# The last half chunk of batch 0 in a fused attention and feed-forward kernel: two TensorE transposes become DMA transposes, and its numerators move from step 10 to step 29

## The chip, the cores and the metric

The kernel runs on one core of a Trainium2 chip. The metric is the device time of one execution in microseconds (us). Nine executions of the kernel before gave a median of 250.71 us, from 249.87 to 252.09. One of them was taken by the hardware profiler; all views below are of that execution. TensorE is called PE (PEld is its weight load), VectorE is DVE, ScalarE is ACT, GpSimd is POOL and SyncE is SP.

## What is computed

Linear attention for 8 batches of 8 heads, 576 positions and 64 channels, and then a feed-forward net on the 4608 resulting tokens of width 512:

```python
theta = np.pi / 2.0 * pos / S
phi(x) = concat([relu(x) * cos(theta), relu(x) * sin(theta)])   # 128 features
kv  = einsum('bhsf,bhsd->bhfd', phi(k), v);  z = sum_s phi(k)
num = einsum('bhsf,bhfd->bhsd', phi(q), kv)
den = einsum('bhsf,bhf->bhs', phi(q), z) + 1e-6
x   = (num / den) transposed to [token, 512]
out = ((x @ w1) * (x @ w2)) @ w3 @ w_out
```

The kernel multiplies w3 and w_out once, into `w34b`, and uses that for all tokens.

## The kernel before, in words

**Tiling.** A batch's 576 positions are cut into five chunks: four of 128 rows and one of 64 rows, chunk 4, called the half chunk here. The tokens of all batches, in order, are cut into nine tiles of 512 for the feed-forward net. Batch 0 has 576 tokens, so its chunks 0 to 3 fill tile 0, and its half chunk is the first 64 columns of tile 1.

**What one chunk of queries goes through.** `features` (L258) makes the 128 features of each head in `qp`: DVE makes the cosine half (L263), ACT the sine half (L267). Then the features have to stand on the partitions: `q_tr` (L321) does it by eight PE transposes into PSUM (L326) and a copy into `qpT` (by DVE, L328, or by ACT, L329); in other places `prep_q` (L277) issues a DMA transpose from SP (L281). `num` (L343) multiplies the features with the batch's `kvs`, eight matmuls of 65 columns (L355) that give numerators and denominators in PSUM, and DVE divides: denominator (L371), reciprocal (L372), product (L373) into `xblk`. Last, `x_tr` (L391) turns `xblk` into the columns of `xT` that the net reads: by four PE transposes (L407) and a copy (L409), or by a DMA transpose from SP (L403), which batches from 2 on and chunk 3 of batch 1 use.

**What sets the order.** The program is laid out by hand. `ffn_groups(t)` (L446) is a generator for token tile t; it issues a group of PE work (four matmuls of 512 columns for the most part) and yields. After the g-th group everything in `slots[g]` is issued (L650 to L655), and `at(s, ...)` (L549) puts work there. Tile 0 has groups, or steps, 0 to 39. Steps 0 to 15 form the products with w1 and w2 (L452), steps 16 to 31 the product of w3 and w_out (`w34_mm`, L225, matmul L230), two steps for each of eight blocks `jp`; steps 32 to 39 the output product (L522). Tile 1 begins after step 39. Each engine runs its own instructions in the order in which they were issued, and waits by semaphores for what others give it. So a step number fixes the place in each engine's queue, not a time; an engine with nothing queued before an instruction can run it as soon as its data are there.

**Around the change.** The half chunk's features are made at step 6, `q_tr(0, 4)` stands at step 8, `num(0, 4)` at 10 and `x_tr(0, 4)` at 12 (L613 to L618). The transposes of the eight w3 blocks, `w3_tr` (L215, PE transposes L218 and a DVE copy L220), stand at steps 13, 15, 17, 19, 22, 24, 26 and 28 (L620); block 4 is the one at step 22. Batch 1's query features and its `q_tr` calls start at steps 29 and 31 (L623 to L626).

**Loads.** Nearly all loads are issued from POOL, and they convert float32 to bf16. `other_loads` (L197) issues the later ones in this order: the rest of w1 and w2, blocks 0 and 1 of w3, w_out, blocks 2 and 3 of w3, the keys of batch 1, then blocks 4 and 5 in one transfer and 6 and 7 in another (L142); step 7 adds queries and values of batch 1 and queries of batch 2 (L614). SP issues two loads of keys at the start and then nothing until batch 1's first DMA transpose at step 31.

Of the kernel before, what the change touches and what calls it, by code (L numbers as in the profile page):

```python
# [20 lines left out]
ROWS = [128, 128, 128, 128, 64]  # L21


def columns_of(b, c):


    if b % 2 == 0:
        return 128 * c
    return 0 if c == 4 else 64 + 128 * c


def out_rows(b, c):

    if c < 4:
        return slice(0, 128)
    return slice(64, 128) if b % 2 == 0 else slice(0, 64)
# [32 lines left out]
def kernel(  # L69
# [11 lines left out]
    nc = tc.nc  # L81
# [29 lines left out]
    def load(b, which, part=None):  # L111
        for name in which:
            src = {"k": k, "v": v, "q": q}[name]
            if part != 1:
                raw[b, name] = ld.tile([P, H, NCH, D], BF16, name=name + "s",
                                       bufs=2 if name == "q" else 1)
                nc.gpsimd.dma_start(
                    out=raw[b, name][0:64, :, :, :].rearrange("p h j d -> p h (j d)"),
                    in_=src[b, :, 0:320, :].rearrange("h (p j) d -> p h (j d)", j=5))
            if part != 0:  # L120
                nc.gpsimd.dma_start(
                    out=raw[b, name][64:128, :, 0:4, :].rearrange("p h j d -> p h (j d)"),
                    in_=src[b, :, 320:S, :].rearrange("h (p j) d -> p h (j d)", j=4))
# [25 lines left out]
    q0 = raw[0, "q"] = ld.tile([P, H, NCH, D], BF16, name="qs", bufs=2)  # L149
# [8 lines left out]
    def feature_buffers(i):  # L158

        va = const.tile([P, NCH, H, D + 2], BF16, name=f"va{i}")  # L160
        nc.vector.memset(va[:, :, :, D:D + 1], 1.0)
        nc.vector.memset(va[64:128, 4, :, 0:D], 0.0)
        va_bufs.append(va)
        for name, bufs in (("kp", kp_bufs), ("qp", qp_bufs)):
            fp = const.tile([P, NCH, H, F], BF16, name=f"{name}{i}")
            nc.vector.memset(fp[64:128, 4, :, :], 0.0)
            bufs.append(fp)
# [68 lines left out]
    def order_of(b):  # L236

        return [0, 1, 2, 3, 4] if b % 2 == 0 else [4, 0, 1, 2, 3]

    def dma_q(b):  # L240

        return order_of(b)[5 if b < 1 else 3 if b == 1 else 0:]

    feat = {}

    def feat_of(b):
        if b not in feat:
            feat[b] = (kp_bufs[b % 2], qp_bufs[b % 2], va_bufs[b % 2])
        return feat[b]
# [3 lines left out]
    def att_of(b):  # L253
        if b not in att:
            att[b] = {"qpT": phi.tile([P, H, S], BF16, name="qpT"), "x": {}}
        return att[b]

    def features(b, dst, src, c, cos=True, sin=True, scalar_heads=H):  # L258

        R = ROWS[c]  # L260
        at = c if b == 0 else NCH + c
        if cos:
            nc.vector.tensor_scalar(out=dst[:R, c, :, 0:D], in0=src[:R, :, c, :], scalar1=0.0,  # L263
                                    scalar2=cosv[:R, at:at + 1], op0=ALU.max, op1=ALU.mult)
        if sin:
            n = scalar_heads
            nc.scalar.activation(out=dst[:R, c, 0:n, D:F], in_=src[:R, 0:n, c, :], func=ACTF.Relu,  # L267
                                 scale=sinv[:R, at:at + 1], bias=0.0)
            if n < H:
                nc.vector.tensor_scalar(out=dst[:R, c, n:H, D:F], in0=src[:R, n:H, c, :],  # L270
                                        scalar1=0.0, scalar2=sinv[:R, at:at + 1],
                                        op0=ALU.max, op1=ALU.mult)

    def prep_k(b, c):
        features(b, feat_of(b)[0], raw[b, "k"], c)

    def prep_q(b, c):  # L277
        features(b, feat_of(b)[1], raw[b, "q"], c)
        if c in dma_q(b):
            R = ROWS[c]  # L280
            nc.sync.dma_start_transpose(out=att_of(b)["qpT"][:, :, ds(columns_of(b, c), R)],  # L281
                                        in_=feat[b][1][:R, c].rearrange("p h f -> p (h f)"))

    def prep_v(b, c):
        R = ROWS[c]
# [35 lines left out]
    def q_tr(b, c, evac=True):  # L321
        R = ROWS[c]
        qp = feat[b][1]
        pst = ps_tr.tile([P, 8, 128], BF16, name="pst")
        for h in range(H):
            nc.tensor.transpose(pst[:, h, :], qp[:, c, h, :], identb[:])  # L326
        dst, src = att_of(b)["qpT"][:, :, ds(columns_of(b, c), R)], pst[:, :, 0:R]
        on_vector = lambda: nc.vector.tensor_copy(out=dst, in_=src)  # L328
        on_scalar = lambda: nc.scalar.copy(out=dst, in_=src)  # L329
        if evac:  # L330
            on_vector()
        return on_vector, on_scalar
# [10 lines left out]
    def num(b, c, chain=True, in_two=False):  # L343
        rows = out_rows(b, c)
        R = ROWS[c]
        at = columns_of(b, c) - rows.start
        qpT, kvs = att[b]["qpT"], att[b]["kvs"]
        if b == 0 and c == 0:
            nt = ps_first.tile([P, 2, 512], FP32, name="pfirst")
        else:  # L350
            pool = more_att[0] if more_att and order_of(b).index(c) % 2 == 0 else ps_att
            nt = None if in_two else pool.tile([P, 2, 512], FP32, name="pnum")
        banks = [ffn_tile(), ffn_tile()] if in_two else [nt[:, g, :] for g in range(2)]
        for h in range(H):
            nc.tensor.matmul(banks[h // 4][:, ds((h % 4) * 65, 65)], lhsT=qpT[:, h, ds(at, 128)],  # L355
                             rhs=kvs[:, h, :], start=True, stop=True)
        if b < 2:
            rows, R = slice(0, P), P
        if in_two:
            parts = [(slice(g, g + 1), t[rows, 0:260].rearrange("p (g h e) -> p g h e", g=1, e=65))  # L360
                     for g, t in enumerate(banks)]
        else:
            parts = [(slice(0, 2), nt[rows, :, 0:260].rearrange("p g (h e) -> p g h e", e=65))]
        xblk = sm.tile([P, 2, 4, D], BF16, name="xblk", bufs=4)
        att[b]["x"][c] = xblk

        def normalize():
            den = sm.tile([P, 2, 4], FP32, name="den")
            for g, n4 in parts:
                G = g.stop - g.start  # L370
                nc.vector.tensor_scalar_add(out=den[rows, g], in0=n4[:, :, :, 64], scalar1=1e-6)  # L371
                nc.vector.reciprocal(out=den[rows, g], in_=den[rows, g])  # L372
                nc.vector.tensor_tensor(out=xblk[rows, g], in0=n4[:, :, :, 0:D],  # L373
                                        in1=den[rows, g].unsqueeze(3).to_broadcast([R, G, 4, D]),
                                        op=ALU.mult)

        if chain:
            normalize()
        return normalize
# [11 lines left out]
    def x_tr(b, c, by_vector=False):  # L391
        R, rows = ROWS[c], out_rows(b, c)
        xblk = att[b]["x"].pop(c)
        xf = xblk[:].rearrange("p g h d -> p (g h d)")
        if b % 2 == 0:
            slot = S * b + 128 * c
        else:
            slot = S * b + (0 if c == 4 else 64 + 128 * c)
        t, o = divmod(slot, 512)
        if t not in xT:  # L400
            xT[t] = xtp.tile([P, 4, 512], BF16, name="xT")
        if b >= 2 or (b == 1 and c == 3):
            nc.sync.dma_start_transpose(out=xT[t][:, :, ds(o, R)], in_=xf[rows])  # L403
            return
        pst = ps_tr.tile([P, 8, 128], BF16, name="pst")
        for kc in range(4):
            nc.tensor.transpose(pst[:, kc, :], xf[:, ts(kc, 128)], identb[:])  # L407
        copy = nc.vector.tensor_copy if by_vector else nc.scalar.copy
        copy(out=xT[t][:, :, ds(o, R)], in_=pst[:, 0:4, rows])  # L409
# [31 lines left out]
    def ffn_tile():  # L441
        pool = ps_ffn[ffn_tiles[0] // 2 % 2]
        ffn_tiles[0] += 1
        return pool.tile([P, 512], FP32, name="ffnps")
# [104 lines left out]
    def at(s, *calls):  # L549
        slots[s] += calls  # L550
# [34 lines left out]
    q0f = feat[0][1]  # L585
    features(0, q0f, q0, 0, scalar_heads=4)
    next(kv_steps)
    prep_q(0, 1)
    idle_mms(2)
    q_tr_halves(0, 0)  # L590
    prep_q(0, 2)
    idle_mms(1)
    num(0, 0)
# [16 lines left out]
    at(1, lambda: x_tr(0, 1, by_vector=True), lambda: q_tr(0, 3, evac=False)[1](), lambda: num(0, 2))  # L610
    at(3, lambda: x_tr(0, 2), lambda: num(0, 3))
    at(5, lambda: x_tr(0, 3))
    at(6, lambda: prep_q(0, 4))  # L613
    at(7, lambda: load(1, "qv"), lambda: load(2, "q"))  # L614
    at(8, lambda: q_tr(0, 4))
    at(10, lambda: num(0, 4))
    at(11, lambda: feature_buffers(1))
    at(12, lambda: x_tr(0, 4))  # L618

    for jp, s in enumerate((13, 15, 17, 19, 22, 24, 26, 28)):  # L620
        at(s, lambda jp=jp: w3_tr(jp))
# [65 lines left out]
```

## Time and profile before

| What | Value |
|---|---|
| median of nine executions | 250.71 us |
| the profiled execution | 250.59 us |
| its span, first to last instruction | 248.8 us |
| around the span | 1.8 us |
| PE busy | 240.3 us, 1855 matmuls recorded |
| DVE busy, ACT busy, POOL busy | 138.5, 130.6, 93.4 us |
| granted TensorE clock, mean | 0.999 |
| moved by DMA | 41.04 MB, mean 165 GB/s |
| DMA transposes, `qpT` and `xT` | 32 and 31, median 5.0 and 4.9 us from issue to landing |

The page gives busy times by engine, the span in 40 slices, the chain of work that ended last, the costliest groups of instructions and the DMA issues. Beside it one can ask the trace for the instructions of a stretch in order of time (the timeline), for who waited for whom (the waits), for the chain piece by piece, for the DMA issues of a stretch with their time to landing, and for busy time and bytes by stretch of time (the windows). Matmuls overlap in the pipeline, so the step from one start to the next, and not the length of one record, tells what a matmul costs; the chain is cut that way.

### The profile page before, as it was taken

How to read it: one execution, taken by the hardware profiler on the slowest of the kernel's cores; microseconds unless marked ns; L12 is line 12 of the kernel's file. 1: busy time of each engine (PE TensorE's matmuls, PEld its weight loads, DVE VectorE, ACT ScalarE, POOL GpSimd, SP SyncE). 2: the span in 40 equal slices, each digit the busy share in tenths (PEclk: the TensorE clock that was granted, in tenths of full speed). 3: DMA queues.
4: the chain of work that ended last, by engine and by line, in shares of the span. 5: the costliest groups of instructions: out<-in, count | busy, mean ns of one | idle time of the engine just before them, and what ended most of it. 6: DMA issues, size and time to landing. Idle time of an engine off the chain costs nothing.

```text
span 248.8 us, 5036 instructions
## 1 busy us (share of the span) xinstructions
PE 240.3 (97%) x1855; PEld 131.3 (53%) x1884; DVE 138.5 (56%) x337; ACT 130.6 (52%) x267; POOL 93.4 (38%) x195
## 2 busy tenths in 40 slices
PE   8999999999999999999999999999999999999993
PEld 3579555466965445455544545455445544444442
DVE  7775753648977454655765674577464643403320
ACT  2675315667934963576448545854575234334322
POOL 7755331214412351218123621472242009785000
PEclk9999999999999999999999999999999999999999
DMA  6999999999999979999999999999999427997025
GB/s 192 186 194 202 206 205 205 198 162 140 167 144 154 151 120 149 137 124 199 165 166 183 188 92 204 206 166 154 152 196 147 91 42 210 289 302 237 0 44 128
DMA packets 83897, 41.04 MB, mean 165 GB/s; under 512 B 51488, under 2 KB 80416, under 8 KB 83872
## 3 DMA queue, kind: packets, MB, share of 16 engines
q0 software_dynamic: 35456, 27.20, 71.3%
q1 hardware_dynamic: 48256, 13.38, 36.6%
q8 instruction: 15, 0.25, 0.4%
q10 hardware_dynamic: 160, 0.13, 0.2%
q14 instruction: 10, 0.08, 0.1%
HBM read 38.80 MB, written 9.44 MB: 194 GB/s over the span
## 4 chain that ended last, share of the span: by engine, by line
PE 84%; DMA 9%; DVE 3%; issue 1%; POOL 1%; ACT 0%; ACTq 0%; POOLq 0%; SPq 0%; DVEq 0%
PE ffnps L452 46%; PE ffnps L522 21%; PE ffnps L230 6%; DMA qpT<-qp 4%; PE pnum L355 4%; DMA qs<-in_q_dram 3%; PE pnum L295 3%; DMA xT<-xblk 2%; PE pst L218 2%; PE pst L326 1%; PE pst L407 1%; DVE qp L263 1%; DVE xblk L373 1%; DVE abT L509 1%; POOL vs L127 0%
## 5 line engine op out<-in xcount | busy, mean ns | idle before, releaser
L452 PE MATMUL ffnps<-xT,w2b 128*128 128x512 bf16 (+2 forms) x340 | 75.3, 344 | 0.3
L452 PE MATMUL ffnps<-xT,w1b 128*128 128x512 bf16 (+2 forms) x331 | 74.1, 343 | 0.6
L509 DVE TENSOR_TENSOR abT<-asb,ffnps 128x512 bf16<-128x512 bf16 x64 | 43.9, 686 | 51.0 <-PE ffnps L452 49.1
L522 PE MATMUL ffnps<-w34b,abT 128*128 128x512 bf16 x271 | 63.7, 379 | 0.4
L505 ACT CAST asb<-ffnps 128x512 bf16<-128x512 f32 x64 | 37.4, 584 | 50.9 <-PE ffnps L452 46.1
L557 POOL COPY seen<-mark 1x1 bf16<-1x1 bf16 x50 | 9.0, 180 | 97.8 <-ACT mark L555 97.8
L452 PEld LDWEIGHTS <-w2b 128*128 128x128 bf16 x344 | 30.8, 98 | 26.5
L452 PEld LDWEIGHTS <-w1b 128*128 128x128 bf16 x344 | 30.7, 98 | 26.2 <-DMA xT<-xblk 0.5
L522 PEld LDWEIGHTS <-abT 128*128 128x128 bf16 x280 | 26.0, 98 | 27.9 <-DVE abT L509 0.2
L529 ACT COPY osb<-ffnps 128x512 f32<-128x512 f32 x35 | 20.5, 585 | 33.9 <-PE ffnps L522 33.5
L267 ACT ACTIVATE qp<-qs,sinv 128x512 bf16<-128x512 bf16 (+2 forms) x40 | 28.1, 714 | 1.4 <-DMA qs<-in_q_dram 1.4
L373 DVE TENSOR_TENSOR xblk<-pnum,den 128x512 bf16<-128x512 f32 (+1 forms) x37 | 25.6, 691 | 1.3
L267 ACT ACTIVATE kp<-ks,sinv 128x512 bf16<-128x512 bf16 (+1 forms) x35 | 24.9, 717 | 2.5 <-DMA ks<-in_k_dram 2.5
L437 POOL DMA_DIRECT2D out_dram<-osb x42 | 22.3, 537 | 3.4 <-issue 3.3
L355 PEld LDWEIGHTS <-qpT 128*128 128x128 bf16 x320 | 15.3, 98 | 9.5 <-DMA qpT<-qp 1.0
L287 POOL COPY va<-vs 128x512 bf16<-128x512 bf16 (+1 forms) x30 | 18.0, 634 | 6.2 <-DMA vs<-in_v_dram 6.2
L371 DVE TENSOR_SCALAR den<-pnum 128x8 f32<-128x8 f32 (+1 forms) x37 | 6.0, 163 | 22.8 <-PE pnum L355 22.7
L263 DVE TENSOR_SCALAR qp<-qs,cosv 128x512 bf16<-128x512 bf16 (+1 forms) x40 | 17.8, 451 | 0.7 <-DMA qs<-in_q_dram 0.7
L355 PE MATMUL pnum<-kvs,qpT 128*128 128x65 bf16 x296 | 15.8, 194 | 0.6 <-DMA qpT<-qp 0.5
L230 PE MATMUL ffnps<-woutb,w3T 128*128 128x512 bf16 x62 | 15.2, 380 | 0.1
L295 PEld LDWEIGHTS <-kp 128*128 128x128 bf16 x280 | 11.4, 98 | 4.1
L263 DVE TENSOR_SCALAR kp<-ks,cosv 128x512 bf16<-128x512 bf16 (+1 forms) x35 | 12.9, 378 | 0.8 <-DMA ks<-in_k_dram 0.8
(86 smaller groups left out, 183.5 us busy)
## 6 DMA issues: line engine op xcount, KB each, us to landing
out_dram<-osb POOLq DMA_DIRECT2D x16, 256.0 KB, 4.5
out_dram<-osb POOLq DMA_DIRECT2D x24, 128.0 KB, 3.8
qs<-in_q_dram POOLq DMA_DIRECT2D x9, 256.0 KB, 7.7
ks<-in_k_dram POOLq DMA_DIRECT2D x7, 320.0 KB, 6.5
qs<-in_q_dram POOLq DMA_DIRECT2D x7, 320.0 KB, 6.4
vs<-in_v_dram POOLq DMA_DIRECT2D x7, 320.0 KB, 5.7
ks<-in_k_dram POOLq DMA_DIRECT2D x7, 256.0 KB, 7.0
vs<-in_v_dram POOLq DMA_DIRECT2D x7, 256.0 KB, 4.8
```

What stands on the lines that cost most here:

```text
L230: nc.tensor.matmul(acc[:, :], lhsT=w3T[:, lc, :], rhs=woutb[:, lc, :], start=(lc == 0), stop=(lc == 7))
L263: nc.vector.tensor_scalar(out=dst[:R, c, :, 0:D], in0=src[:R, :, c, :], scalar1=0.0, scalar2=cosv[:R, at:at + 1], op0=ALU.max, op1=ALU.mult)
L267: nc.scalar.activation(out=dst[:R, c, 0:n, D:F], in_=src[:R, 0:n, c, :], func=ACTF.Relu, scale=sinv[:R, at:at + 1], bias=0.0)
L295: nc.tensor.matmul(kvt[:, h // 4, ds((h % 4) * 65, 65)], lhsT=kp[:, c, h, :], rhs=va[:, c, h, 0:D + 1], start=(i == 0 and h % 4 == 0), sto ...
L355: nc.tensor.matmul(banks[h // 4][:, ds((h % 4) * 65, 65)], lhsT=qpT[:, h, ds(at, 128)], rhs=kvs[:, h, :], start=True, stop=True)
L373: nc.vector.tensor_tensor(out=xblk[rows, g], in0=n4[:, :, :, 0:D], in1=den[rows, g].unsqueeze(3).to_broadcast([R, G, 4, D]), op=ALU.mult)
L437: on.dma_start(out=rows[:, :, cols], in_=osb[64 * i:64 * i + rows.shape[0], :, cols])
L452: nc.tensor.matmul(out, lhsT=w[:, kc, ts(jc, 128)], rhs=x[:, kc, tok], start=(kc == 0), stop=(kc == 3))
L505: nc.scalar.copy(out=asb[:], in_=aT[:, :])
L509: nc.vector.tensor_mul(out=abT[:, jc, :], in0=asb[:], in1=bT[:, :])
L522: nc.tensor.matmul(ops[:, :], lhsT=abT[:, jc, ts(ms, 128)], rhs=w34b[:, jc, :], start=(jc == 0), stop=(jc == 7))
L529: nc.scalar.copy(out=osb[:, ms % 2, :], in_=ops[:, :])
```

## The change

The half chunk of batch 0 no longer goes through PE transposes. A function `transpose_q` holds the DMA transpose of `prep_q`, and is called for the half chunk at step 23. The features stay at step 6. The numerators go to step 29, and the transpose of the normalized half chunk, now also at step 29, is a DMA transpose from SP. At step 29 both are registered ahead of `prep_q(1, 4)`, so they are issued before it.

```diff
+    def transpose_q(b, c):
+        R = ROWS[c]
+        nc.sync.dma_start_transpose(out=att_of(b)["qpT"][:, :, ds(columns_of(b, c), R)],
+                                    in_=feat[b][1][:R, c].rearrange("p h f -> p (h f)"))
...
         features(b, feat_of(b)[1], raw[b, "q"], c)
         if c in dma_q(b):
-            R = ROWS[c]
-            nc.sync.dma_start_transpose(out=att_of(b)["qpT"][:, :, ds(columns_of(b, c), R)],
-                                        in_=feat[b][1][:R, c].rearrange("p h f -> p (h f)"))
+            transpose_q(b, c)
...
-        if b >= 2 or (b == 1 and c == 3):
+        if b >= 2 or (b, c) in ((0, 4), (1, 3)):
             nc.sync.dma_start_transpose(out=xT[t][:, :, ds(o, R)], in_=xf[rows])
             return
...
-    at(6, lambda: prep_q(0, 4))
+    at(6, lambda: features(0, q0f, q0, 4))
+    at(23, lambda: transpose_q(0, 4))
     at(7, lambda: load(1, "qv"), lambda: load(2, "q"))
-    at(8, lambda: q_tr(0, 4))
-    at(10, lambda: num(0, 4))
+    at(29, lambda: num(0, 4))
     at(11, lambda: feature_buffers(1))
-    at(12, lambda: x_tr(0, 4))
+    at(29, lambda: x_tr(0, 4))
```

## The prediction

> **What bounds the kernel now.** I read the page first, then PE's waits, then the chain piece by piece around the change, then weight loads, DMA issues and windows there. The page says that PE sets the time:
>
> ```profile
> PE 240.3 (97%) x1855; PEld 131.3 (53%) x1884; DVE 138.5 (56%) x337; ACT 130.6 (52%) x267; POOL 93.4 (38%) x195
> ```
>
> From 15 us to the tail PE hardly idles; its waits over the whole span, as the matmuls see them, hold one DMA:
>
> ```profile
> PE unread L179 <- DVE zeros L155: 1.2, 1, 1.2
> PE pnum L355 <- DMA qpT<-qp: 0.5, 1, 0.5
> ```
>
> So PE work taken away should come off the end, unless PE then has to wait. The chain from 25 to 52 us (start, length, what) holds the instructions that the change takes away or moves:
>
> ```profile
> 25.61 0.45 PE pst L326 x8
> ...
> 27.78 0.26 PE pnum L355 x8
> ...
> 29.77 0.22 PE pst L407 x4
> ...
> 37.37 0.45 PE pst L218 x8
> 37.82 0.65 PE ffnps L230 x3
> 38.47 0.05 issue
> 38.52 1.89 PE ffnps L230 x8
> 40.41 0.62 PE pst L218 x8
> ...
> 47.83 2.69 PE ffnps L230 x12
> ```
>
> The first three are `q_tr(0, 4)`, `num(0, 4)` and `x_tr(0, 4)`. The piece at 38.52 is the odd one: eight 512-column matmuls take 1.73 us in the other pieces and 1.89 here, though nothing else is in it. The end belongs to the next instruction, `w3_tr(4)` at step 22. The weight loads say why:
>
> ```profile
> 40.40 0.45 PEld L218 LDWEIGHTS <-w3b 128*128 128x128 bf16 x8 [0.49 <-DMA w3b<-in_moe_w_dram]
> ```
>
> PE was ready at 38.52 + 1.73 = 40.25 and went on at 40.41: it waited 0.16 us for blocks 4 and 5 of w3. POOL issued that load at 24.95, and the issues around that time give its 15.4 us to landing, so it landed at about 40.36:
>
> ```profile
> w3b<-in_moe_w_dram POOLq DMA_DIRECT2D x1, 512.0 KB, 15.4
> ```
>
> It is late because the DMA engines are behind. The windows (length, busy times, clock, DMA share, GB/s) show a full queue from 15 us to 52:
>
> ```profile
> 25.00:33.00 8.00, 7.93 (x60) 4.45 (x61) 6.08 (x13) 2.76 (x6) 2.43 (x4) 1.00 1.20 207
> 33.00:41.00 8.00, 7.95 (x61) 4.41 (x60) 2.67 (x4) 2.38 (x4) 3.03 (x5) 1.00 1.23 207
> 67.40:69.80 2.40, 2.40 (x41) 2.23 (x39) 1.90 (x5) 1.35 (x3) 0.00 (x0) 1.00 0.96 212
> 140.00:150.00 10.00, 9.37 (x91) 5.09 (x92) 6.33 (x16) 4.48 (x10) 2.71 (x7) 1.00 1.47 121
> ```
>
> The first two are loads alone, the third DMA transposes alone, the fourth a mixture. PE and DMA thus meet within 0.16 us at `w3_tr(4)`. This is where the forecast is decided.
>
> **PE work, ahead of step 22.** Removed: 8 transposes, 0.45 us, and 4, 0.22 us. Moved behind it: the 8 matmuls of `num`, 0.26 us. Together 0.93 us less, so PE would be ready for `w3_tr(4)` at 40.25 - 0.93 = 39.32. But the load lands at 40.36 at the earliest. Of the 0.93 us nothing is gained there; instead PE waits over a microsecond. The DVE copy of 0.42 us and the ACT copy of 0.38 us that go away lie beside PE work; nothing waited for them, and they count zero.
>
> **The new `qpT` transpose.** The features' last half ends on ACT at 22.59 + 0.72 = 23.31. SP has nothing queued since its two loads at the start, so step 23 does not hold it back: it will issue at about 23.4, long before PE reaches step 23, and right into the load queue. Its own landing is no concern: landings of `qpT` run from 2.7 to 9.6 us, so it is there by 33, and `num` wants it at about 49. Its cost is what it takes from the loads. It writes 64 x 1024 bf16 = 131 KB, and the w3 load's data come after it. In the row of transposes alone the engines moved 212 GB/s, in the row of loads alone 207, so 131 KB push the load by about 0.63 us. Here the Trainium skill gives another price: the page DMA: Bandwidth & Descriptors, section Anatomy of one DMA — SWDGE (gpsimd) path, fits a fixed 2.0 us, which is latency, and bytes over 436 GB/s, fitted to its other kind of DMA. By it I would estimate 0.30 us, and a sum below 0.3% of the time. No row of this trace moves transposes at that pace, so 0.63 stands. Bounds: zero, if the loads are held by what they read from memory and the engines have room for a transfer inside SBUF; and 1.5 us, from the mixed row: at 121 instead of 207 GB/s ten microseconds lost 10 x (1 - 121/207) = 4.2 us, and about five half-chunks' worth of transposes (two and a half of 262 KB) fell in it, 0.8 each on top of 0.63. I take 0.63, as the two unmixed rows agree and most of the stretch has one short transpose among loads. Below zero is excluded: nothing leaves the DMA queue.
>
> **What the push does.** Blocks 4 and 5 then land at 40.99 and PE goes on at 41.04, 0.63 later than before. It stands for 1.7 us in all since 25 us, some of it already at the first w34 matmuls, where w_out (issued at 19.31, 13.0 to landing, so 32.3 + 0.6) is wanted by PE at 33.47 - 0.93 = 32.54; that wait is inside the same 1.7. No row shows the clock after a gap of this size; the page TensorE: Matmul & The Clock Gate, section Why this matters for your kernels, sets its warning at gaps of about 3 us, so I charge nothing. The last two w3 blocks, issued at 26.25 and 16.6 us to landing, come at 42.85 + 0.63, and `w3_tr(6)` stands at 45.12 + 0.63: no second wait.
>
> **Step 29.** `num` now stands behind the first four of the twelve matmuls at 47.83, that is at 48.69 + 0.63, and adds its 0.26 us to a PE that has no gap from there on. Its 8 matmuls wait for nothing new: `kvs` and PSUM have long been free. On DVE the division now runs ahead of batch 1's query features. Before, from the start of `num` (27.78) to the end of the division (28.59 + 0.69) was 1.50 us. The first features (0.34 us) are then done 1.84 us behind the start of `num`; PE wants them for `q_tr(1, 4)` 0.26 + 1.83 = 2.09 us behind it (before: 50.52 against 48.69). So 0.25 us cover it; if that cover goes, PE waits the difference, at most a few tenths. Behind them on DVE wait the value copies and the `qpT` copies, which PE wants 2 us later and more. I count zero. SP carries the half chunk's `xT` transpose (65 KB) ahead of batch 1's first `qpT` transpose: an issue takes about 1.2 us of SP, from about 50.8 to 52.0, and the next one is ready at 52.28 + 0.9. At the longest landing seen, 8.6 us, `xT` is there at 59.4, and tile 1 begins at 61.51 + 0.9. It pushes loads by 0.3 us whose data PE wants microseconds later. POOL issues as before; its loads are paced by landings and shift with them.
>
> **Sum.** 0.63 + 0.26 = 0.89 us on the profiled execution's 250.59: 251.5. That execution lies 0.12 us below the median of the nine, so I forecast 250.71 + 0.89 = 251.6.
>
> **Rivals.**
>
> *The load stops binding (not slower).* All hangs on one landing. If in most executions blocks 4 and 5 land ahead of PE, the PE work taken away counts in full: -0.93 + 0.26 = -0.67 us, 250.0. For the whole of it the load, 0.63 later than it would be, must be there by PE's 39.32, so 1.7 us sooner than in this trace; the change breaks even if the load lands 1.0 us sooner than in this trace (39.3, which the push of 0.63 and 0.05 of start and the 0.26 bring back to 40.25). For it: one execution is all that I see, and the nine times differ by 2.2 us. Against it: the queue was full from its start, at a steady 194 to 218 GB/s in the windows from 15 to 52 us, and 1.7 us of 40 would need 4% more.
>
> *The transpose hides in the loads.* Then PE is pinned at 40.41 as before, and only the 0.26 of step 29 is added: 251.0. For it: the two kinds read different memories. Against it: the mixed row is slower, not faster.
>
> *Mixing costs more.* As in the mixed row, 1.5 + 0.26 = 1.8 us: 252.5. For it: the 9.6 us landing in that row. Against it: one half transpose against several whole ones there.
>
> **How the numbers follow.** The likeliest case, a push of 0.4 to 1.0 us: 0.52 in 10, with 251.4 to 252.0. Mixing worse: 0.14. Hidden or nearly: 0.16. Load not binding: 0.18. About 0.3%, 0.75 us, is what a measurement of this kernel can tell from no change; the likeliest case lies just above it, so I give three quarters of it to slower and the rest to no change; mixing goes to slower; hidden goes to no change; of the last case 0.08 to faster, since -0.67 is at the border, 0.10 to no change. That makes slower 0.53, same 0.39, faster 0.08. The range takes in the full gain and most of the worse mixing: 250.0 to 252.6.
>
> **What would show it.** Right: the `qpT` transpose issued at about 23.4 us; blocks 4 and 5 landing near 41.0; weight loads for L218 waiting about a microsecond or more for `w3b`; `num` at 49.3; tile 1 beginning 0.9 us later than 61.51. Wrong: no such wait, or a landing at or ahead of 40.36 (the push), or PE waiting at step 31 on `qp` (the DVE order), or at tile 1's start on `xT`.

## The result and the profile after

The changed kernel takes 252.12 us (median of 17 executions), the kernel before 250.75 (54 executions). The ratio is 1.0054, 95% interval 1.0037 to 1.0072: slower by 1.35 us, between 0.93 and 1.8. The profiled execution of the changed kernel took 251.56 us, span 249.7, against 250.59 and 248.8. Below, a ratio is turned into us with 250.7, and all stage times are from the profiled execution of each kernel. In the changed kernel and its variants the lines behind `prep_q` are 3 higher: L326 is L329, L355 is L358.

Three of PE's waits over the span (who waited for what: us, times, longest):

```profile
PE kva L315 <- DVE va L290: 1.2, 1, 1.2
PE pst L218 <- DMA w3b<-in_moe_w_dram: 1.0, 1, 1.0
PE ffnps L230 <- DMA woutb<-in_moe_w_out_dram: 0.8, 1, 0.8
```

The second and third are new waits of PE for loads. (The first lies ahead of the change, is 0.2 us in the kernel before, and is gone into at the end.) The chain around them:

```profile
25.13 16.38 DMA w3b<-in_moe_w_dram
41.51 0.05 issue
41.55 0.62 PE pst L218 x8
...
48.98 0.65 PE ffnps L230 x3
49.63 0.05 issue
49.69 0.42 PE pnum L358 x8
50.10 1.73 PE ffnps L230 x8
51.83 0.52 PE pst L329 x8
```

From 25.13 us up to `w3_tr(4)` the chain is now one transfer, the load of w3 blocks 4 and 5. It lands at 41.51 instead of 40.36, and `w3_tr(4)` starts at 41.55 instead of 40.41. At 49.69 stand the numerators of step 29, the only new piece between there and tile 1. The weight loads, with the idle time before them, show both waits:

```profile
33.40 1.42 PEld L230 LDWEIGHTS <-w3T 128*128 128x128 bf16 x8 [0.91 <-DVE abT L512]
...
41.55 0.45 PEld L218 LDWEIGHTS <-w3b 128*128 128x128 bf16 x8 [1.52 <-DMA w3b<-in_moe_w_dram]
```

and in PE's own timeline the first of the two carries its right name:

```profile
33.43 1.89 PE L230 MATMUL ffnps<-woutb,w3T 128*128 128x512 bf16 x7 [0.76 <-DMA woutb<-in_moe_w_out_dram]
```

What pushes the loads is in SP's timeline and the DMA issues (the last figure is us to landing): the transpose goes out at 23.45, among loads, and takes 9.1 us.

```profile
23.45 1.29 SPq L276 DMA_TRANSPOSE qpT<-qp  x1
51.37 1.17 SPq L406 DMA_TRANSPOSE xT<-xblk  x1
```

```profile
qpT<-qp SPq DMA_TRANSPOSE x1, 9.1
```

The windows of the same stretches as before (length, busy times, clock, DMA share, GB/s):

```profile
25.00:33.00 8.00, 7.62 (x47) 3.84 (x46) 5.45 (x12) 2.62 (x5) 2.10 (x3) 1.00 1.21 203
33.00:41.00 8.00, 7.04 (x43) 3.56 (x44) 2.00 (x4) 2.38 (x4) 3.40 (x5) 1.00 1.23 206
```

PE is idle for 0.38 us of the first window and 0.96 of the second, where before it was idle for 0.07 and 0.05.

### The profile page after: what moved, and what is told of

The parts are those of the page before. It is cut to its first block, busy times and chain, and to the rows that moved or that the text cites. A ratio compares the mean times of both kernels' runs of the same rounds, so it can differ in the third digit from the quotient of the medians.

```text
span 249.7 us, 5017 instructions
## 1 busy us (share of the span) xinstructions
PE 239.0 (96%) x1843; PEld 130.4 (52%) x1872; DVE 139.2 (56%) x336; ACT 130.2 (52%) x266; POOL 93.4 (37%) x195
## 4 chain that ended last, share of the span: by engine, by line
PE 77%; DMA 17%; DVE 2%; issue 1%; POOL 1%; ACT 0%; ACTq 0%; POOLq 0%; SPq 0%; DVEq 0%
PE ffnps L455 40%; PE ffnps L525 24%; DMA w3b<-in_moe_w_dram 7%; DMA qpT<-qp 4%; PE pnum L358 4%; DMA w2b<-in_moe_w_dram 3%; DMA qs<-in_q_dram 3%; PE ffnps L230 3%; PE pnum L298 3%; PE pst L218 1%; DVE qp L263 1%; PE pst L329 1%; POOL vs L127 0%; PE pst L410 0%; PE ffnps L541 0%
## 5 line engine op out<-in xcount | busy, mean ns | idle before, releaser
L455 PE MATMUL ffnps<-xT,w2b 128*128 128x512 bf16 (+2 forms) x340 | 75.3, 344 | 0.3
L455 PE MATMUL ffnps<-xT,w1b 128*128 128x512 bf16 (+2 forms) x332 | 74.2, 343 | 0.5
L455 PEld LDWEIGHTS <-w2b 128*128 128x128 bf16 x344 | 31.0, 98 | 27.3
L455 PEld LDWEIGHTS <-w1b 128*128 128x128 bf16 x344 | 30.7, 98 | 25.9
L358 PEld LDWEIGHTS <-qpT 128*128 128x128 bf16 x320 | 15.3, 98 | 9.3 <-DMA qpT<-qp 0.9
L263 DVE TENSOR_SCALAR qp<-qs,cosv 128x512 bf16<-128x512 bf16 (+1 forms) x40 | 19.0, 483 | 0.5 <-DMA qs<-in_q_dram 0.5
L358 PE MATMUL pnum<-kvs,qpT 128*128 128x65 bf16 x296 | 15.8, 194 | 0.6 <-DMA qpT<-qp 0.4
L230 PE MATMUL ffnps<-woutb,w3T 128*128 128x512 bf16 x61 | 15.1, 379 | 0.9 <-DMA woutb<-in_moe_w_out_dram 0.8
```

Of the source, the lines that this page charges most:

```text
L230: nc.tensor.matmul(acc[:, :], lhsT=w3T[:, lc, :], rhs=woutb[:, lc, :], start=(lc == 0), stop=(lc == 7))
L455: nc.tensor.matmul(out, lhsT=w[:, kc, ts(jc, 128)], rhs=x[:, kc, tok], start=(kc == 0), stop=(kc == 3))
```

## The experiments

The theory: the DMA transpose of the queries pushes loads that PE waits for (the push), so the PE work taken away ahead of step 22 is worth nothing, and the numerators at step 29 add to the end. The rival: the time is lost at and behind step 29, by the order of the work on DVE, SP and PE there.

**One transpose added to the kernel before.** Nothing else is changed.

```diff
+    spare = const.tile([P, H, 64], BF16, name="spare")
+    def extra():
+        nc.sync.dma_start_transpose(out=spare[:, :, :],
+                                    in_=feat[0][1][:64, 4].rearrange("p h f -> p (h f)"))
-    at(6, lambda: prep_q(0, 4))
+    at(6, lambda: prep_q(0, 4), extra)
```

> The kernel before with one DMA transpose more: the half chunk's query features also go to a spare tile that nothing reads, issued where the changed kernel issues its own; PE's work is that of before. Push theory (the transpose delays the load of w3 blocks 4 and 5, and PE waits for it): the load lands 0.6 to 1.0 us later than in the kernel before, PE's weight loads for w3_tr(4) wait as much longer, and the time is 0.6 to 1.0 us above before. Rival (the loss comes at step 29, from the order of DVE and PE there): no difference, within 0.2 us.

Measured: ratio 1.0018 (1.0000 to 1.0037), 0.45 us slower (0.0 to 0.9). Its weight loads:

```profile
41.23 0.45 PEld L218 LDWEIGHTS <-w3b 128*128 128x128 bf16 x8 [1.22 <-DMA w3b<-in_moe_w_dram]
```

40.40 before, 41.23 here, with PE's work unchanged: the push is there by itself, 0.83 us. In this execution the loads ahead of the transpose landed 0.19 us earlier than before (the last w2 load at 24.48 against 24.67); measured from that load, the landing of blocks 4 and 5 (41.19 against 40.36) is 1.02 later. The time rose by less than expected, though the interval takes in most of what was expected.

**Two transposes added to the kernel before.** The same with two issues into a spare tile twice as large (`for i in range(2)`).

> The kernel before with two DMA transposes more, both of the half chunk's query features into a spare tile that nothing reads. Push theory: in the profile, the start of w3_tr(4) is pushed by about twice the 0.7 us that one such transpose gave, 1.3 to 1.6 us, and the time rises by 0.8 to 1.4 us. If one transpose's push was chance or was hidden: less than 0.8 us at w3_tr(4).

Measured: ratio 1.0079 (1.0052 to 1.0105), 2.0 us slower (1.3 to 2.6), above the range expected, whose upper end the interval just reaches.

```profile
43.23 0.34 PEld L218 LDWEIGHTS <-w3b 128*128 128x128 bf16 x6 [1.22 <-DMA w3b<-in_moe_w_dram]
```

`w3_tr(4)` is pushed by 2.83 us, of which 0.33 is a later start (the last w2 load lands at 25.00): about 1.25 per transpose, more than the 0.7 to 0.8 expected. In its PE timeline, w_out too is late now:

```profile
35.41 0.81 PE L230 MATMUL ffnps<-woutb,w3T 128*128 128x512 bf16 x3 [1.55 <-DMA woutb<-in_moe_w_out_dram]
```

So the push grows with the number of transposes, and it is real time.

**The query transpose back on PE, the rest as in the changed kernel.**

```diff
-    at(23, lambda: transpose_q(0, 4))
+    at(8, lambda: q_tr(0, 4))
```

> The changed kernel with the query half chunk transposed by PE again at step 8; numerators and output transpose (by DMA) stay at step 29. Push theory: no transpose among the loads before 40 us, so w3 blocks 4 and 5 land as in the kernel before; PE is ready 0.5 us sooner but waits for them, and only the 0.26 us of the numerators at step 29 are added: 0.2 to 0.4 us above before, about 1 us below the changed kernel. Rival (step 29): as slow as the changed kernel, 1.3 us above before.

Measured: ratio 1.0012 (0.9993 to 1.0030), 0.3 us slower (-0.2 to 0.75).

```profile
40.57 0.45 PEld L218 LDWEIGHTS <-w3b 128*128 128x128 bf16 x8 [0.80 <-DMA w3b<-in_moe_w_dram]
```

All of step 29 is here as in the changed kernel, and most of the loss is gone: the load lands at about 40.5 again, and `w3_tr(4)` starts 0.17 us later than before. PE, with 0.48 us less to do up to there, waits. This speaks against the rival.

**All of the half chunk's PE work ahead of `w3_tr(4)`.** Only the query transpose is by DMA.

```diff
-    at(6, lambda: features(0, q0f, q0, 4))
-    at(23, lambda: transpose_q(0, 4))
-    at(29, lambda: num(0, 4))
-    at(29, lambda: x_tr(0, 4))
+    at(6, lambda: features(0, q0f, q0, 4), lambda: transpose_q(0, 4))
+    at(18, lambda: num(0, 4))
+    at(21, lambda: x_tr(0, 4))
...
-        if b >= 2 or (b, c) in ((0, 4), (1, 3)):
+        if b >= 2 or (b, c) == (1, 3):
```

> The changed kernel with the numerators at step 18 and the output transpose by PE at step 21, so that all of the half chunk's PE work stands ahead of w3_tr(4); only the query transpose is by DMA, issued at 23.4 us as in the changed kernel. Push theory: that PE work fits into the time in which PE waits for blocks 4 and 5 anyway, so w3_tr(4) starts as in the changed kernel, about 1 us later than before, but the 0.26 us of step 29 are gone: 0.6 to 1.0 us above before. Rival (step 29): no loss, within 0.2 us of before.

Measured: ratio 1.0038 (1.0018 to 1.0058), 0.95 us slower (0.45 to 1.45). In its chain,

```profile
41.89 0.05 issue
41.93 0.62 PE pst L218 x8
...
49.36 2.69 PE ffnps L230 x12
52.05 0.45 PE pst L329 x8
```

step 29 is empty (twelve matmuls in one piece), and `w3_tr(4)` starts at 41.93. With nothing moved to step 29 the loss is still there, so the rival falls. That it is 0.4 us smaller than the changed kernel's fits the 0.26 us of the numerators, but the intervals overlap.

**The transpose later.** Features and transpose at step 21, numerators and `x_tr` at step 30.

```diff
-    at(6, lambda: features(0, q0f, q0, 4))
-    at(23, lambda: transpose_q(0, 4))
-    at(29, lambda: num(0, 4))
-    at(29, lambda: x_tr(0, 4))
+    at(21, lambda: features(0, q0f, q0, 4), lambda: transpose_q(0, 4))
+    at(30, lambda: num(0, 4), lambda: x_tr(0, 4))
```

> The changed kernel with the half chunk's features and its query transpose both at step 21 (so that SP can't issue the transpose before about 39 us) and with numerators and output transpose at step 30. Push theory: the transpose now comes behind most of the load of w3 blocks 4 and 5, which lands within 0.3 us of where it does in the kernel before; w_out too; PE waits at w3_tr(4) until about 40.5, then adds 0.26 us: 0.3 to 0.6 us above before, 0.8 us or so below the changed kernel. If the transpose takes 9 us among the loads, PE may wait for it at step 30, at most some tenths. Rival (step 29): 1.3 us above before.

Measured: ratio 1.0011 (0.9990 to 1.0031), 0.3 us slower (-0.25 to 0.8). SP issues the transpose at 40.24, the load lands at 40.75, w_out at 32.5 as before. The median is where the push theory put it, at the lower edge; the interval ends at 0.8 us, below the rival's 1.3. The profiled execution was 2 us slower than that of before. 0.65 of it is there at step 31, 0.35 of that from a later start; the rest came later, at single waits between 79 and 135 us, most of them for a load or a DMA transpose, where the kernel is not changed.

**Blocks 4 and 5 of w3 ahead of batch 1's keys.** The same edit on three kernels: the changed one, the one before, and the late version.

```diff
-        load(1, "k")
-        for jp in range(4, 8, 2):
-            load_w3(jp, 2)
+        load_w3(4, 2)
+        load(1, "k")
+        load_w3(6, 2)
```

> The changed kernel with the load of w3 blocks 4 and 5 issued ahead of the keys of batch 1 instead of behind them. Push theory: the load lands some 2.5 us sooner, PE no longer waits for it, and the 0.67 us of PE work taken away shows: 0.5 to 0.8 us below before, some 2 us below the changed kernel; batch 1's keys land 2.5 us later, which their step 22 and 23 can take. Rival (step 29): the load's place changes nothing, 1.3 us above before.

> The kernel before with the load of w3 blocks 4 and 5 issued ahead of the keys of batch 1. Push theory: only the 0.16 us that PE waited for this load in the kernel before are gained, so 0.0 to 0.3 us below before, and slower than the changed kernel with the same edit by 0.5 us or so. Rival (step 29): no difference from before, and faster than the changed kernel with the same edit by 1.3 us.

> The late version with the load of w3 blocks 4 and 5 issued ahead of the keys of batch 1 as well. Both waits that ate the gain in the profiles so far (for w_out at the first w3 x w_out products, and for blocks 4 and 5) should be gone: 0.5 to 0.8 us below before, with PE ahead of the kernel before by 0.9 us at step 22 and by 0.7 from step 30 on, unless blocks 6 and 7, which the late transpose now pushes, become the next wait at step 26 (then 0.2 to 0.5 below). If PE work taken away were worth nothing for another reason: no difference from before.

Measured, against before: the changed kernel with it 1.0002 (0.9977 to 1.0026), 0.05 us; before with it 0.9997 (0.9981 to 1.0013), -0.1 us; the late version with it 0.9967 (0.9934 to 0.9999), -0.8 us (-1.7 to -0.0). The first missed its expectation, and PE's waits say why:

```profile
PE ffnps L230 <- DMA woutb<-in_moe_w_out_dram: 0.8, 1, 0.8
```

The wait for blocks 4 and 5 is gone (they land at 38.3), but w_out, pushed to 33.25, had already taken the gain at the first product of w3 and w_out. That is the second load, wanted before the one that this edit moves. The edit still took back most of the 1.35 us. Between the first two, which the push theory put 0.5 us apart, no difference can be told. In the late version the transpose goes out behind w_out and blocks 4 and 5, and neither is waited for:

```profile
38.98 0.86 PE ffnps L230 x4
39.84 0.45 PE pst L218 x8
...
48.92 0.26 PE pnum L358 x8
49.18 0.86 PE ffnps L230 x4
50.05 0.45 PE pst L329 x8
```

This is its chain, all PE but for one DVE copy in the part left out. The starts of `w3_tr(4)` are compared in PE's timeline, the late version's first, then that of the kernel before with the same order of loads:

```profile
39.68 0.61 PE L218 MATMUL pst<-identb,w3b 128*128 128x128 bf16 x8
```

```profile
40.60 0.61 PE L218 MATMUL pst<-identb,w3b 128*128 128x128 bf16 x8
```

The two executions began alike (first product, L455 and L452, at 16.06 and 16.05), and neither waits for a load here. So the difference, 0.92 us, is the 0.93 of PE work that was taken away and moved. At batch 1's first `q_tr` it is 50.05 against 50.70 in the chains, 0.65: the 0.67 of PE work that is gone for good. Against the kernel before in its old order of loads, which began 0.36 us sooner (15.70), `w3_tr(4)` comes 0.73 sooner (39.68 against 40.41); with the start that is 1.09, the 0.93 and the 0.16 that PE waited there. The median of the late version agrees. It is clearly below the changed kernel, but its interval ends just at the kernel before and overlaps that of the kernel before with the same order of loads; that it is ahead of that one is shown by the two traces, up to tile 1 (60.88 against 61.54), and not by the times.

**w_out in halves as well.** The first half ahead of w3 block 1 and the second behind it, on top of the edit above; on the changed kernel and on the one before.

```diff
-        for jp in range(2):
-            load_w3(jp, 1)
-        load_wout()
+        load_w3(0, 1)
+        load_wout(0)
+        load_w3(1, 1)
+        load_wout(1)
```

> The changed kernel (query transpose issued at 23.4 us, numerators at step 29) with other loads arranged so that none of them is wanted before it lands: w_out comes in two halves, the first ahead of w3 block 1 and the second behind it, and blocks 4 and 5 ahead of the keys of batch 1. Push theory: the transpose still pushes the loads by 0.7 to 1.0 us, but PE waits for none of them by more than 0.3 us; 0.4 to 0.8 us below before, some 2 us below the changed kernel. Rival (what is issued at step 29 costs the time): no gain over the changed kernel, 1.3 us above before.

> The kernel before with the same arrangement of loads (w_out in two halves, blocks 4 and 5 ahead of the keys). It is the other half of the comparison: only the 0.16 us of waiting are there to be gained, so 0.0 to 0.3 us below before, and 0.3 to 0.7 us slower than the changed kernel with this arrangement. If the arrangement itself were what gains, this one would be as fast as that.

Measured: the changed kernel with it 0.9984 (0.9958 to 1.0010), -0.4 us; before with it 1.0017 (0.9990 to 1.0045), 0.4 us. Each alone can't be told from before, and the second's median lies above the range expected of it. But the changed kernel, its transpose still at 23.7 us and step 29 as it was, is below its own 1.0054 by more than both intervals: with no load wanted late, no cost of the edit is left that the times could show. In the chains, with the later starts (0.35 and 0.37 at the first product) taken out, batch 1's first `q_tr` comes 0.70 us sooner than before with the change (50.17 against 50.52) and 0.17 sooner without it (50.72): the difference is 0.53, near the 0.67 of the sum. The executions' times scatter too much to show it.

**The changed kernel once more.**

> The changed kernel itself once more, on the chip of the two runs above, for a comparison on one chip and a second profile. Push theory: 0.9 to 1.6 us above before; in the profile a wait for w_out at the first w3 x w_out products, a wait of about a microsecond for blocks 4 and 5, and no wait on features, xT or SP from step 29 to the start of tile 1.

Measured: ratio 1.0099 (1.0070 to 1.0128) from six executions, 2.5 us slower (1.8 to 3.2), above what was expected, and above the first measurement's interval but for its edge. In this profile the start was late and PE came to the first w34 products 0.9 us behind before, not ahead of it, yet:

```profile
41.73 0.45 PEld L218 LDWEIGHTS <-w3b 128*128 128x128 bf16 x8 [0.92 <-DMA w3b<-in_moe_w_dram]
```

PE again waited for blocks 4 and 5 and went on within 0.2 us of the first profile. The expected wait for w_out was not there, since PE itself was late.

## Why the prediction was right, and what it mis-sized

The way and the mechanism were right: slower, by a load that the new transpose pushes and that PE waits for, and by the numerators behind it. The size was low: 0.89 us lies below the interval of the first measurement, 0.93 to 1.8, and of the second.

**What bounds the kernel** was right: PE, and at `w3_tr(4)` PE and the load together. One reading behind it was wrong, though its result holds. The chain's piece of 1.89 us doesn't show the wait. It stands behind a short "issue" piece, where the record of a matmul is missing; there the chain counts from a start and not from the end of a predecessor, which makes the piece 0.16 longer. The chain of the kernel before with w_out in halves has the same piece, and PE waits for no load there (its L232 is L230):

```profile
38.83 0.05 issue
38.89 1.89 PE ffnps L232 x8
40.78 0.45 PE pst L220 x8
```

What holds is the sum of starts: eight matmuls from 38.52 take 1.73, and `w3_tr(4)` starts at 40.41, 0.16 later than it could. That the two figures of 0.16 are the same is chance.

**PE work ahead of step 22 counts nothing** was right, and the experiments show both halves of it: while the loads are late it is lost; in the late version with blocks 4 and 5 ahead, the whole of it is seen at `w3_tr(4)`.

**The new transpose** is the term that was mis-sized. The issue at "about 23.4" came at 23.45. The push was put at 0.63 us, from 131 KB at the rate of transposes alone or loads alone. The landing moved by 41.51 - 40.36 = 1.15 us. The last w2 load, whose data come ahead of the transpose, was already 0.18 late in this execution (24.85 against 24.67; the two loads ahead of it, landed by 23.52, were as late), so the push is 0.97. The first window says where most of it went: moved bytes fall from 207 to 203 GB/s while 131 KB of them are the transpose, so the loads lost (207 - 203) x 8 + 131 = 163 KB there, 0.8 us at 207 GB/s. Measured in the same way, from that w2 load, the push is 1.02 with the single added transpose, 1.32 in the changed kernel's second profile, 1.39 with all of the half chunk's PE work ahead, and 2.50 with two added transposes. The two profiles in the old order of loads with no transpose among them, the query transpose back on PE and the late one, give 0.28 and 0.14, so a few tenths of such a figure can be chance.

The agreement of the two unmixed rows, on which 0.63 rests, was chance too. The row of transposes alone ends in a stretch where almost nothing was left to move:

```profile
67.40:69.20 1.80, 1.80 (x36) 1.69 (x34) 1.80 (x5) 1.35 (x3) 0.00 (x0) 1.00 1.26 278
69.20:69.80 0.60, 0.60 (x8) 0.54 (x6) 0.10 (x1) 0.00 (x0) 0.00 (x0) 1.00 0.08 12
```

So transposes alone moved 278 GB/s, not 212, and 131 KB at that rate would be 0.47 us. Among loads the transpose took about twice that. The 436 GB/s of the Trainium skill (DMA: Bandwidth & Descriptors, section Anatomy of one DMA — SWDGE (gpsimd) path), by which it would have been 0.30, is further off. The mixed row's 1.5 us was above all that was measured, but that row too has 1.2 us, from 144.0 to 145.2, at 41 GB/s. What makes a transpose dearer among loads than alone was not tried.

**What the push does.** The wait for w_out was told and put at about 0.4 us (32.9 against 32.54); it was 0.76. It mattered only in the experiments, where it hid the gain until it was dealt with. No second wait at `w3_tr(6)`: right. The clock stayed at 1.00 over both waits.

**Step 29.** The numerators add 0.26 us; from `w3_tr(4)` (1.15 later) to batch 1's first `q_tr` (1.38 later, 51.74 against 50.35) 0.24 were added. (The 0.42 of their piece in the chain is the same gap in the records as above: the next matmul starts 0.25 behind them, at 49.94.) The DVE order was counted zero: `q_tr(1, 4)` stands 0.07 us behind the end of the eight matmuls before it (51.74 in the timeline, against 49.94 + 1.73). SP and `xT`: the transpose was issued at 51.37 and landed 6.2 us later, 57.5, ahead of tile 1 at 62.73. Right.

**The sum**, 0.89 us, became 1.38 at tile 1 (62.73 against 61.35 in the timeline): 0.97 push, 0.24 numerators, and 0.18 of a later start. The median moved by 1.35. That the profiled execution ended only 0.97 behind, near the forecast, is luck. The shift falls by 0.18 us at 132 us, where the kernel before waits for an `xT` transpose and the changed one need not; by 0.13 near 149, where both wait for a `qpT` transpose; and by about 0.1 behind the last products.

**The rivals.** The load did not stop binding: in all profiles with a transpose among the early loads and the loads in their old order, PE waited at `w3_tr(4)`. The transpose did not hide. Mixing cost more than the likeliest case, not as much as the third rival.

**What stays open.** One added transpose cost 0.45 us in time where its push was about 1 us. In its profile the 0.84 us by which tile 1 came late are there unchanged at 131 us. Then 0.18 are taken back at 132, and 0.69 near 149, where the kernel before waits for a `qpT` transpose and this execution does not:

```profile
149.49 0.43 PE L355 MATMUL pnum<-kvs,qpT 128*128 128x65 bf16 x8 [0.53 <-DMA qpT<-qp]
```

```profile
149.46 0.42 PE L355 MATMUL pnum<-kvs,qpT 128*128 128x65 bf16 x8
```

So an early push can be hidden by a later wait, in one execution and not in the next. How often that happens, and why the changed kernel's second measurement gave 2.5 us where the first gave 1.35, was not tried; single executions of one kernel differ by 2 us and more.

## What to carry to other kernels

PE work is worth its time only if PE's next wait does not take it: walk from the edit along the engine to the next instruction that waits for a load, and then to the one after it, since each load that lands late takes the gain anew. A DMA transpose is not free because its data are wanted late: an idle queue issues it as soon as its data are there, and among saturated loads it pushes each of them, here by about 1 us for 131 KB. Where the loads are ordered so that the ones wanted first come first, or the transpose is made to come behind them, the cost goes: the changed kernel, 1.35 us slower, can't be told from the kernel before once its loads are reordered, and a version with the transpose late and one load moved came out 0.8 us faster, with an interval that ends just at no gain.

## What was not expected of the hardware

The start of an execution is less steady than what follows. In the second profile of the changed kernel PE waited 2.0 us for the keys' features, and the granted clock then was 0.80 from 9 to 12 us and 0.72 from 12 to 16, where the kernel before has 1.00 in both:

```profile
9.00:12.00 3.00, 1.42 (x30) 1.42 (x30) 2.19 (x8) 1.56 (x3) 1.46 (x2) 0.80 1.86 179
12.00:16.00 4.00, 3.71 (x43) 2.62 (x41) 2.50 (x9) 2.58 (x6) 0.00 (x0) 0.72 1.49 195
16.00:20.00 4.00, 3.65 (x67) 3.32 (x67) 2.81 (x9) 2.95 (x4) 3.51 (x7) 1.00 1.55 192
```

The clock was at half from shortly after that wait, which ended at 10.58, for 3.4 us:

```profile
10.83:14.24 3.41, 3.19 (x47) 2.85 (x45) 1.60 (x7) 2.08 (x5) 1.13 (x2) 0.50 1.62 190
```

In the first profile PE waited 1.2 us at the same matmuls, and in that of the kernel before with blocks 4 and 5 ahead 1.7 us; there the clock stayed at 1.00. The prediction took the 3 us of the Trainium skill (TensorE: Matmul & The Clock Gate, section Why this matters for your kernels) as the length of a gap that matters; here the clock fell behind one of 2.0 us. It is one execution, and whether the gap alone did it was not tried. PE's first query transpose (L342) began at 13.44, in the first profile at 12.01; at `w3_tr(4)` this execution was within 0.2 us of the first one, since PE waited for the load in both.
